# Order of the routing decision: exponentials ahead of the one-hot, gates one unit behind the ranks

## The chip, the cores and the metric

The kernel runs on one core of one Trainium2 chip. The metric is the device time of one execution in microseconds. The core has a matrix engine (PE, with its weight loads listed apart as PEld), a vector engine (DVE), a scalar engine (ACT), GpSimd (POOL) and a queue engine (SP) that issues most transfers.

## What is computed

Attention inside clusters, followed by a mixture of experts. There are 4 batches of 768 tokens with 8 heads of 64 columns; every token then has 512 features, and there are 3072 tokens.

```python
q_assign = argmax(q_n @ c_n); k_assign = argmax(k_n @ c_n)     # 16 clusters a head
scores   = where(q_assign == k_assign, scale * q @ k.T, -1e9)
x        = softmax(scores) @ v                                 # [3072, 512]

g_logits = x @ w_group                     # 4 groups
g_idx, g_w = argmax(g_logits), softmax(g_logits)[g_idx]
e_logits = x @ w_expert[g_idx]             # 4 experts in the group
e_idx, e_w = argmax(e_logits), softmax(e_logits)[e_idx]
out[token] = g_w * e_w * (relu(x @ w1[g, e]) @ w2[g, e])       # F = 1024
```

## The kernel before

**Attention** is cut into units: 32 heads with 9 units each, one unit being 512 columns of scores. In each unit PE makes the fine scores (tile `psf`, lines 346 and 347), ACT takes their exponential (`p`, L351), POOL subtracts the rounded part of it (`pl`, L353), and five units later PE multiplies both with V (L372 and L373). Beside that run coarse scores (`psc`, L304) for a head further ahead, whose maxima DVE takes (L307). All other work is hung beside units: `beside(g)` runs the jobs that are due in unit `g`, and a generator that says `yield` goes on one unit later. Generators that take a bank of the pool `psm` queue for turns. What is written in one unit is put into each engine's stream by a scheduler, so the order within a unit is not the order of the code.

**Routing.** When a batch's last head is done, `logits` multiplies its rows with the router's weights (L596 transposes, L604 products, L610 sums into `lg`: 6 blocks of 128 tokens, 20 logits each). Then `decide` runs for the batch. It takes the maxima of each 4 logits (`rmx`, L628), marks the first maximum (`req` L630 and L631, `rmw` L633, `roh` L635), multiplies group and expert to the one-hot of 16 experts (`roe`, L643), lets PE count with it how many earlier tokens chose each expert (L655 to L659, into `psm`), and adds that rank to the expert's start (`rps`, `rds`). The result `rdi` (L667) is each token's row in a table in HBM. Beside that it makes the gate: differences to the maxima (`rdf`, L638), exponentials (L639 on ACT), their sums (`rse`), and the reciprocal into `pay` (L650). Each of a batch's six table writes (L678, an indirect transfer issued by POOL) carries `pay` to the rows in `rdi`; they are issued one at a time, five units apart (four in the third batch).

**What hangs on the decisions.** After the third batch's decision (`then`) the generator `first` picks the fullest expert (L803 to L813), loads its weights (L760) from the number in `f0i`, splits them beside the units (L780 to L788), and, when all three batches' table writes have landed, reads that expert's rows of the table (`tabA`, L836), turns them into indices on DVE (`idA`, L842) and gathers the tokens with POOL (L916). The last batch's decision comes after attention, beside the first expert's products (L954, L976). Its table writes must land before SP reads the table (`tb`, L1096), behind which the other experts' weights wait in SP's queue (L760).

The lines that place the work are these:

```python
yield PSM, 1, 1            # a turn for a bank of psm, one unit on
...
if early: early()          # last batch: the experts' order
if then: then()            # third batch: starts first()
for c in range(T):
    for _ in range(1 if early else 4 if then else 5):
        yield
    ... nc.gpsimd.indirect_dma_start(out=self.table, ...)
```

Of the kernel before, what the change touches and what calls it, by code (L numbers as in the profile page):

```python
# [13 lines left out]
F32 = mybir.dt.float32  # L14
I32 = mybir.dt.int32
AF = mybir.ActivationFunctionType
ALU = mybir.AluOpType
AX = mybir.AxisListType
# [4 lines left out]
P = 128  # L23
SQ = 16.0
XS = 128.0
WS = 32.0
YS = 64.0
WRS = 16.0
# [500 lines left out]
class Router:  # L529
# [90 lines left out]
    def decide(self, b, early=None, then=None):  # L620
        nc, sm, E = self.nc, self.sm, self.E
        lg = self.lg[b]
        T = lg.shape[1]
        t0 = b * T
        G = T * 5
        lv = lg.rearrange("p t (g x) -> p (t g) x", x=4)
        mx = sm.tile([P, G], F32, name="rmx")
        nc.vector.tensor_reduce(out=mx, in_=lv, axis=AX.X, op=ALU.max)  # L628
        eq = sm.tile([P, G, 4], F16, name="req")
        nc.vector.tensor_tensor(out=eq, in0=lv, in1=mx.broadcast_to([P, G, 4]), op=ALU.is_ge)  # L630
        nc.vector.tensor_tensor(out=eq, in0=eq, in1=self.desc[:, 0:G], op=ALU.mult)  # L631
# [2 lines left out]
        oh = sm.tile([P, T, 5, 4], F16, name="roh")  # L634
        nc.vector.tensor_tensor(out=oh.rearrange("p t g x -> p (t g) x"), in0=eq, in1=mw.broadcast_to([P, G, 4]), op=ALU.is_equal)  # L635
        yield
        df = sm.tile([P, G, 4], F32, name="rdf")
        nc.vector.tensor_tensor(out=df, in0=lv, in1=mx.broadcast_to([P, G, 4]), op=ALU.subtract)  # L638
        nc.scalar.activation(out=df, in_=df, func=AF.Exp, scale=1.0 / (XS * WRS))  # L639
        se = sm.tile([P, T, 5], F32, name="rse")  # L640
        nc.vector.tensor_reduce(out=se.rearrange("p t g -> p (t g)"), in_=df, axis=AX.X, op=ALU.add)
        oe = sm.tile([P, T, 4, 4], F16, name="roe")
        nc.vector.tensor_tensor(out=oe, in0=oh[:, :, 1:5], in1=oh[:, :, 0].broadcast_to([P, T, 4, 4]), op=ALU.mult)  # L643
        ss = sm.tile([P, T, 4], F32, name="rss")
        nc.vector.tensor_tensor(out=ss, in0=se[:, :, 1:5], in1=oh[:, :, 0], op=ALU.mult)
        es = sm.tile([P, T], F32, name="res")
        nc.vector.tensor_reduce(out=es, in_=ss, axis=AX.X, op=ALU.add)
        nc.vector.tensor_scalar(out=es, in0=es, scalar1=1e-9, scalar2=None, op0=ALU.add)
        nc.vector.scalar_tensor_tensor(out=es, in0=se[:, :, 0], scalar=1e-9, in1=es, op0=ALU.add, op1=ALU.mult)
        nc.vector.reciprocal(out=self.pay[:, t0:t0 + T, 1], in_=es)  # L650
        yield PSM, 1, 1
        o16 = oe.rearrange("p t g x -> p (t g x)")
        rk = self.psm.tile([P, 512], F32, name="psm")
# [12 lines left out]
        di = sm.tile([P, T], I32, name="rdi", bufs=2)  # L666
        self.last["v"] = nc.vector.tensor_copy(out=di, in_=ds_)  # L667
        nc.vector.tensor_tensor(out=self.cb, in0=rk[:, W:W + E], in1=self.cb, op=ALU.add)
        if early:
            early()  # L670
        if then:
            then()
        for c in range(T):
# [3 lines left out]
            with self.tc.issue_after(self.cfg["lo"].ins) if self.apart and not early and "lo" in self.cfg else ExitStack():  # L677
                d = self.last["p"] = nc.gpsimd.indirect_dma_start(  # L678
                    out=self.table, out_offset=bass.IndirectOffsetOnAxis(ap=di[:, c:c + 1], axis=0),
                    in_=self.pay[:, t0 + c], in_offset=None)  # L680
# [756 lines left out]
```

## Time and profile before

| | |
|---|---|
| Three runs | 776.68, 778.99, 779.47 us (median 778.99) |
| Profiled execution | 779.44 us |
| Its span, first to last instruction | 777.2 us |
| Outside the span | 2.24 us |
| PE, PEld | 730.4 us (94%), 626.4 us (81%) |
| DVE, ACT, POOL | 606.1 (78%), 466.0 (60%), 492.1 us (63%) |
| Attention, then the last decision, then experts | about 0 to 426, 426 to 445, 445 to 777 us |

Busy time is a sum over the whole span, and different stages have different limits. A row of the timeline has start, duration, engine, line, operation, output and input, and in brackets how long the engine sat idle before it and what ended that idle time. Durations of neighbours on one engine overlap a little, since the next instruction begins before the one ahead has written its last result.

### The profile page before, as it was taken

To read this page: it belongs to the slowest core of one execution; us is meant where nothing else is said; L and a number is where in the kernel's file an instruction comes from. 1 tells how busy PE (TensorE), PEld (TensorE's weight loads), DVE (VectorE), ACT (ScalarE), POOL (GpSimd) and SP (SyncE) were. 2 spreads that over 40 slices of the span, in tenths; PEclk is the share of its full clock that TensorE was granted. 3 is DMA by queue.
4 is the path that set the end of the run, shared out by engine and by line. 5 is a ranking of instruction groups with operands and counts; after the bars stand their busy time and mean duration, and the time that the engine had idled before them with its cause. 6 is when DMAs were issued, how large, how long until landed. Compare 5 with 4: busy or idle time off the path is not lost. (4 is left out here: it accounts for less than half of the span.)

```text
span 777.2 us, 26716 instructions
## 1 busy us (share of the span) xinstructions
PE 730.4 (94%) x11086; PEld 626.4 (81%) x11086; DVE 606.1 (78%) x1209; ACT 466.0 (60%) x910; POOL 492.1 (63%) x522
## 2 busy tenths in 40 slices
PE   5899999999999999997989899999999999999992
PEld 3667888878888788886878687888789999999991
DVE  5888978899788998988875466857678888888840
ACT  5557877868777687775885255453444455555440
POOL 9567688779977799776972445434654555565330
PEclk9889999999999999999999999999999999999996
DMA  8756524535344352223312397876688788888700
GB/s 245 199 139 179 145 80 117 166 94 146 91 117 155 94 149 69 55 94 128 93 29 81 86 300 242 271 229 215 210 267 257 226 282 264 266 276 268 228 31 18
DMA packets 80392, 128.28 MB, mean 165 GB/s; under 512 B 8851, under 2 KB 47251, under 8 KB 80264
## 3 DMA queue, kind: packets, MB, share of 16 engines
q1 hardware_dynamic: 74492, 113.12, 48.9%
q0 software_dynamic: 5616, 13.35, 5.1%
q8 instruction: 88, 1.44, 0.8%
q14 instruction: 40, 0.33, 0.2%
q10 hardware_dynamic: 156, 0.03, 0.0%
HBM read 93.20 MB, written 14.11 MB: 138 GB/s over the span
## 5 line engine op out<-in xcount | busy, mean ns | idle before, releaser
L353 POOL TENSOR_TENSOR pl<-p 128x512 f16<-128x512 f32 x278 | 286.0, 1048 | 84.0 <-ACT p L351 79.5
L307 DVE TENSOR_REDUCE mpart<-psc 128x1 f32<-128x512 f32 (+1 forms) x282 | 189.9, 683 | 34.1 <-PE psc L304 34.1
L351 ACT ACTIVATE p<-psf 128x512 f32<-128x512 f32 x288 | 168.5, 594 | 56.4 <-PE psf L347 52.0
L372 PE MATMUL pso<-V,p 128*128 128x65 f16 x1152 | 161.9, 194 | 0.0
L372 PE MATMUL pso<-V,pl 128*128 128x65 f16 x1152 | 161.4, 194 | 0.0
L373 PE MATMUL pso<-V,pl 128*128 128x64 f16 x1152 | 161.2, 192 | 0.0
L373 PE MATMUL pso<-V,p 128*128 128x64 f16 x1152 | 161.1, 192 | 0.0
L346 PE MATMUL psf<-A 82*128 82x384 f16 (+2 forms) x576 | 145.5, 278 | 5.6 <-ACT p L351 4.8
L347 PE MATMUL psf<-B 128*128 128x384 f16 (+2 forms) x576 | 146.0, 278 | 0.0
L373 PEld LDWEIGHTS <-p 128*128 128x128 bf16 x1152 | 112.6, 98 | 21.6 <-issue 0.4
L372 PEld LDWEIGHTS <-p 128*128 128x128 bf16 x1152 | 112.1, 97 | 8.8 <-issue 0.8
L304 PE MATMUL psc<-A 80*128 80x512 f16 (+1 forms) x376 | 109.4, 332 | 4.1 <-DVE mpart L307 2.9
L373 PEld LDWEIGHTS <-pl 128*128 128x128 f16 x1152 | 112.8, 98 | 0.4
L372 PEld LDWEIGHTS <-pl 128*128 128x128 f16 x1152 | 111.2, 97 | 0.3
L957 DVE SCALAR_TENSOR_TENSOR hl<-psh,hh 128x160 f16<-128x160 f32 (+14 forms) x136 | 50.0, 371 | 61.2 <-ACT hh L956 61.0
L956 ACT ACTIVATE hh<-psh 128x160 f16<-128x160 f32 (+14 forms) x136 | 46.4, 346 | 66.5 <-PE psh L954 66.0
L954 PE MATMUL psh<-xT,wh0a 128*128 128x288 f16 (+7 forms) x512 | 74.7, 255 | 0.0
L347 PEld LDWEIGHTS <-B 128*128 128x128 f16 x576 | 57.2, 99 | 16.4 <-issue 8.0
L916 POOL DMA_INDIRECT xg<-xbuf,ri x32 | 40.9, 1279 | 39.6 <-PE psm L926 24.9
L954 PE MATMUL psh<-xT,wh0b 128*128 128x272 f16 (+6 forms) x448 | 65.0, 254 | 0.6 <-ACT xT L928 0.4
L346 PEld LDWEIGHTS <-A 82*128 82x128 f16 x576 | 56.1, 99 | 9.9 <-issue 1.0
L954 PE MATMUL psh<-xT,wl0a 128*128 128x288 f16 (+7 forms) x256 | 64.1, 255 | 0.0
(311 smaller groups left out, 1747.5 us busy)
## 6 DMA issues: line engine op xcount, KB each, us to landing
st<-w SPq DMA_DIRECT2D x128, 512.0 KB
B<-parts SPq DMA_DIRECT2D x64, 192.0 KB
kx<-kT SPq DMA_DIRECT2D x16, 384.0 KB
qx<-qT SPq DMA_DIRECT2D x16, 384.0 KB
vx<-vr SPq DMA_DIRECT2D x16, 384.0 KB
A<-parts SPq DMA_DIRECT2D x32, 192.0 KB
xbuf<-xs SPq DMA_DIRECT2D x4, 1536.0 KB
A<-mk SPq DMA_DIRECT2D x56, 24.0 KB
```

Source lines behind the costliest of these rows:

```text
L304: last["mm"] = nc.tensor.matmul(out=pc[:, off:off + k1 - k0], lhsT=QA[h % 8][0:80, c * P:(c + 1) * P], rhs=KA[h % 8][0:80, k0:k1], start=T ...
L307: nc.vector.tensor_reduce(out=(mp[:, 0, 0:1], mp[:, :, 1], mp[:, 1, 0:1])[i], in_=pc.rearrange("p (a x) -> p a x", a=n), axis=AX.X, op=ALU ...
L346: nc.tensor.matmul(out=o, lhsT=KA[h % 8][0:82, ks], rhs=QA[h % 8][0:82, q0:q1], start=True, stop=False)
L347: nc.tensor.matmul(out=o, lhsT=KBs[h][:, ks], rhs=QBs[h][:, q0:q1], start=False, stop=True)
L351: cfg["exp"] = nc.scalar.activation(out=p32, in_=pf, func=AF.Exp, scale=QK / (SQ * SQ))
L353: lo = (nc.vector if u in (EARLY if h < 2 else DVE_LO[h % 8] if h < NH - 2 else DVE_END) else nc.gpsimd).tensor_tensor(out=pl, in0=p32, in ...
L372: nc.tensor.matmul(out=O[:, col:col + 65], lhsT=p[:, bs], rhs=vh, start=c == 0 and q == 0 and i == 0, stop=False, skip_group_check=True)
L373: nc.tensor.matmul(out=O[:, col:col + 64], lhsT=p[:, bs], rhs=vl, start=False, stop=c == NCH - 1 and i == 1, skip_group_check=True)
L916: self.got = nc.gpsimd.indirect_dma_start(out=xg[0:n].rearrange("p a d -> p (a d)"), out_offset=None, in_offset=bass.IndirectOffsetOnAxis( ...
L954: self.mm = nc.tensor.matmul(out=ph[:, 0:M], lhsT=w[:, k, fs], rhs=xT[:, a, k], start=i == 0, stop=i == 3 * KD - 1)
L956: nc.scalar.activation(out=hh[:, f], in_=ph[:, 0:M], func=AF.Relu)
L957: self.ev = nc.vector.scalar_tensor_tensor(out=hl[:, f], in0=ph[:, 0:M], scalar=0.0, in1=hh[:, f], op0=ALU.max, op1=ALU.subtract)
```

## The change

In `decide`, the differences `rdf` and their exponentials move up, ahead of the comparisons. The sums, the product with the group's one-hot and the reciprocal (`rse`, `rss`, `res`, `pay`) move down behind the ranks, behind a new `yield`; `early()`, `then()` and the table writes follow them. No instruction is added or taken away, and the steps that make the one-hot from the comparisons stay as they are.

```diff
         nc.vector.tensor_reduce(out=mx, in_=lv, axis=AX.X, op=ALU.max)
+
+        df = sm.tile([P, G, 4], F32, name="rdf")
+        nc.vector.tensor_tensor(out=df, in0=lv, in1=mx.broadcast_to([P, G, 4]), op=ALU.subtract)
+        nc.scalar.activation(out=df, in_=df, func=AF.Exp, scale=1.0 / (XS * WRS))
         eq = sm.tile([P, G, 4], F16, name="req")
...
         yield
-        df = sm.tile([P, G, 4], F32, name="rdf")
-        nc.vector.tensor_tensor(out=df, in0=lv, in1=mx.broadcast_to([P, G, 4]), op=ALU.subtract)
-        nc.scalar.activation(out=df, in_=df, func=AF.Exp, scale=1.0 / (XS * WRS))
-        se = sm.tile([P, T, 5], F32, name="rse")
-        nc.vector.tensor_reduce(out=se.rearrange("p t g -> p (t g)"), in_=df, axis=AX.X, op=ALU.add)
         oe = sm.tile([P, T, 4, 4], F16, name="roe")
         nc.vector.tensor_tensor(out=oe, in0=oh[:, :, 1:5], in1=oh[:, :, 0].broadcast_to([P, T, 4, 4]), op=ALU.mult)
-        ss = sm.tile([P, T, 4], F32, name="rss")
-        nc.vector.tensor_tensor(out=ss, in0=se[:, :, 1:5], in1=oh[:, :, 0], op=ALU.mult)
-        es = sm.tile([P, T], F32, name="res")
-        nc.vector.tensor_reduce(out=es, in_=ss, axis=AX.X, op=ALU.add)
-        nc.vector.tensor_scalar(out=es, in0=es, scalar1=1e-9, scalar2=None, op0=ALU.add)
-        nc.vector.scalar_tensor_tensor(out=es, in0=se[:, :, 0], scalar=1e-9, in1=es, op0=ALU.add, op1=ALU.mult)
-        nc.vector.reciprocal(out=self.pay[:, t0:t0 + T, 1], in_=es)
         yield PSM, 1, 1
...
         nc.vector.tensor_tensor(out=self.cb, in0=rk[:, W:W + E], in1=self.cb, op=ALU.add)
+        yield
+
+        se = sm.tile([P, T, 5], F32, name="rse")
+        nc.vector.tensor_reduce(out=se.rearrange("p t g -> p (t g)"), in_=df, axis=AX.X, op=ALU.add)
+        ss = sm.tile([P, T, 4], F32, name="rss")
+        nc.vector.tensor_tensor(out=ss, in0=se[:, :, 1:5], in1=oh[:, :, 0], op=ALU.mult)
+        es = sm.tile([P, T], F32, name="res")
+        nc.vector.tensor_reduce(out=es, in_=ss, axis=AX.X, op=ALU.add)
+        nc.vector.tensor_scalar(out=es, in0=es, scalar1=1e-9, scalar2=None, op0=ALU.add)
+        nc.vector.scalar_tensor_tensor(out=es, in0=se[:, :, 0], scalar=1e-9, in1=es, op0=ALU.add, op1=ALU.mult)
+        nc.vector.reciprocal(out=self.pay[:, t0:t0 + T, 1], in_=es)
         if early:
             early()
```

On DVE, the third batch's decision stands so before, from the maxima to the one-hot (`mpart` are the coarse maxima of L307):

```order
L628 TENSOR_REDUCE rmx<-lg 128x30
L630 TENSOR_TENSOR req<-lg,rmx 128x120
L307 TENSOR_REDUCE mpart_199<-psc 128x2
L631 TENSOR_TENSOR req<-req,desc_502 128x120
L638 TENSOR_TENSOR rdf<-lg,rmx 128x120
L633 TENSOR_REDUCE rmw<-req 128x30
L635 TENSOR_TENSOR roh<-req,rmw 128x120
L307 TENSOR_REDUCE mpart_199<-psc 128x1
L641 TENSOR_REDUCE rse<-rdf 128x30
L643 TENSOR_TENSOR roe<-roh 128x96
```

and so in the changed kernel, whose lines have other numbers:

```order
L628 TENSOR_REDUCE rmx<-lg 128x30
L631 TENSOR_TENSOR rdf<-lg,rmx 128x120
L307 TENSOR_REDUCE mpart_199<-psc 128x2
L634 TENSOR_TENSOR req<-lg,rmx 128x120
L664 TENSOR_REDUCE rse<-rdf 128x30
L635 TENSOR_TENSOR req<-req,desc_502 128x120
L637 TENSOR_REDUCE rmw<-req 128x30
L307 TENSOR_REDUCE mpart_199<-psc 128x1
L639 TENSOR_TENSOR roh<-req,rmw 128x120
L642 TENSOR_TENSOR roe<-roh 128x96
```

`rdf` and `rse` have moved up past the comparisons, but both still stand ahead of `roe`: the same ten instructions in another order. The first two batches read alike.

On DVE, behind the same batch's ranks, `first` stands so before (`ft`, `cntA` and `fm` are its small tiles of 16 experts, `DEN`, `rec` and `pso` belong to the attention head that has just ended):

```order
L667 CAST rdi<-rds 128x6
L803 TENSOR_TENSOR cntA<-cb,ebase 128x16
L388 RECIPROCAL rec<-DEN 128x6
L804 SCALAR_TENSOR_TENSOR ft<-cntA,io 128x16
L391 TENSOR_TENSOR pso<-pso,rec 128x6x64
L805 TENSOR_REDUCE fm<-ft 128x1
L307 TENSOR_REDUCE mpart_199<-psc 128x1
L393 TENSOR_TENSOR xs<-pso,xs 128x6x64
```

and so in the changed kernel:

```order
L659 CAST rdi<-rds 128x6
L671 RECIPROCAL pay<-res 128x6
L388 RECIPROCAL rec<-DEN 128x6
L806 TENSOR_TENSOR cntA<-cb,ebase 128x16
L391 TENSOR_TENSOR pso<-pso,rec 128x6x64
L307 TENSOR_REDUCE mpart_199<-psc 128x1
L393 TENSOR_TENSOR xs<-pso,xs 128x6x64
L807 SCALAR_TENSOR_TENSOR ft<-cntA,io 128x16
```

`pay` has come in behind `rdi`, and two of `first`'s operations have moved behind the coarse maximum. On POOL, each batch's first table write stands one L353 later than before (behind 101 of them instead of 100 in the first batch), with the same spacing behind it, while the gather of L916 keeps its place: between the third batch's sixth write and that gather there are three L353 instead of four. SP's order is the same.

On DVE, the last decision stands so before, from the expert's `hl` (L957) on:

```order
L957 SCALAR_TENSOR_TENSOR hl<-psh,hh 128x288
L649 SCALAR_TENSOR_TENSOR res<-rse,res 128x6
L662 TENSOR_TENSOR rps<-psm,cb 128x96
L650 RECIPROCAL pay<-res 128x6
L663 TENSOR_TENSOR rps<-rps,roe 128x96
L668 TENSOR_TENSOR cb<-psm,cb 128x16
L665 TENSOR_REDUCE rds<-rps 128x6
L1051 TENSOR_TENSOR c_11405<-cb,ebase 128x16
L1087 COPY pb<-pay 128x6
L667 CAST rdi<-rds 128x6
```

and so in the changed kernel:

```order
L960 SCALAR_TENSOR_TENSOR hl<-psh,hh 128x288
L654 TENSOR_TENSOR rps<-psm,cb 128x96
L669 TENSOR_SCALAR res<-res 128x6
L655 TENSOR_TENSOR rps<-rps,roe 128x96
L660 TENSOR_TENSOR cb<-psm,cb 128x16
L657 TENSOR_REDUCE rds<-rps 128x6
L670 SCALAR_TENSOR_TENSOR res<-rse,res 128x6
L1054 TENSOR_TENSOR c_11405<-cb,ebase 128x16
L659 CAST rdi<-rds 128x6
L671 RECIPROCAL pay<-res 128x6
```

The second multiplication of the gate (`res` from `res`) has moved from ahead of `hl` to behind it, `pay` now comes directly behind `rdi`, and the copy `pb` has gone further down.

## Rows read from the trace of the kernel before

**Rows 1.** The page, part 1: the span, and each engine's busy time, share and instructions.

```profile
span 777.2 us, 26716 instructions
PE 730.4 (94%) x11086; PEld 626.4 (81%) x11086; DVE 606.1 (78%) x1209; ACT 466.0 (60%) x910; POOL 492.1 (63%) x522
```

**Rows 2.** PE's waits over the whole span: what waited, for what, us in total, times, longest.

```profile
PE psm L655 <- DVE roe L643: 4.1, 3, 1.4
PE psc L304 <- DVE mpart L307: 2.9, 6, 0.8
...
PE psm L1126 <- DMA tb<-table: 2.8, 1, 2.8
```

**Rows 3.** The timeline of PE between 340 and 372 us, the rows with idle time before them.

```profile
350.70 0.20 PE L655 MATMUL psm<-roe,low 128*128 128x96 f16 x1 [1.35 <-DVE roe L643]
...
355.83 0.38 PE L304 MATMUL psc<-A 80*128 80x256 f16 x2 [0.73 <-DVE mpart L307]
360.17 0.38 PE L304 MATMUL psc<-A 80*128 80x256 f16 x2 [0.69 <-DVE mpart L307]
365.15 0.27 PE L346 MATMUL psf<-A 82*128 82x256 f16 x1 [1.53 <-ACT p L351]
```

**Rows 4.** The timeline of DVE in the third batch's decision.

```profile
346.43 0.85 DVE L630 TENSOR_TENSOR req<-lg,rmx 128x120 f16<-128x120 f32 x1
...
347.80 0.45 DVE L631 TENSOR_TENSOR req<-req,desc 128x120 f16<-128x120 f16 x1
348.18 0.27 DVE L638 TENSOR_TENSOR rdf<-lg,rmx 128x120 f32<-128x120 f32 x1
...
348.67 0.82 DVE L635 TENSOR_TENSOR roh<-req,rmw 128x120 f16<-128x120 f16 x1
...
350.19 0.45 DVE L643 TENSOR_TENSOR roe<-roh 128x96 f16<-128x96 f16 x1
```

**Rows 5.** The timeline of POOL in the same stretch: five L353 in a row.

```profile
345.10 5.43 POOL L353 TENSOR_TENSOR pl<-p 128x512 f16<-128x512 f32 x5 [1.03 <-ACT p L351]
```

**Rows 6.** The same operations and the exponential in all four decisions: count, shortest, median and longest in ns, first and last start in us. The shortest is that of the last decision, in which POOL runs no L353.

```profile
L630 DVE TENSOR_TENSOR req<-lg,rmx x4: 284/852/856, 155.1 to 426.0; 128x120 f16<-128x120 f32 x4
L631 DVE TENSOR_TENSOR req<-req,desc x4: 215/452/452, 156.5 to 426.4; 128x120 f16<-128x120 f16 x4
...
L635 DVE TENSOR_TENSOR roh<-req,rmw x4: 274/816/817, 157.3 to 427.0; 128x120 f16<-128x120 f16 x4
...
L643 DVE TENSOR_TENSOR roe<-roh x4: 257/454/454, 158.9 to 427.3; 128x96 f16<-128x96 f16 x4
...
L639 ACT ACTIVATE rdf<-rdf x4: 303/303/303, 157.1 to 426.5; 128x120 f32<-128x120 f32 x4
```

**Rows 7.** The timeline of DVE behind the third batch's ranks.

```profile
353.65 0.98 DVE L804 SCALAR_TENSOR_TENSOR ft<-cntA,io 128x16 f32<-128x16 f32 x1
...
355.10 0.67 DVE L307 TENSOR_REDUCE mpart<-psc 128x1 f32<-128x512 f32 x1
...
358.34 0.97 DVE L812 TENSOR_TENSOR ft<-ft,oh 128x16 f32<-128x16 f32 x1
...
359.44 0.68 DVE L307 TENSOR_REDUCE mpart<-psc 128x1 f32<-128x512 f32 x1
```

**Rows 8.** ACT and POOL where the first expert's weights arrive.

```profile
363.03 1.06 ACT L780 ACTIVATE wh<-st 128x1024 f16<-128x1024 f32 x1 [1.50 <-DMA st<-w]
364.00 0.58 ACT L787 ACTIVATE psm<-st 128x512 f32<-128x512 f32 x1
...
365.17 2.04 POOL L353 TENSOR_TENSOR pl<-p 128x512 f16<-128x512 f32 x2 [2.00 <-ACT p L351]
```

**Rows 9.** The third batch's sixth table write, the reading of the table and what hangs on it, on POOL, SP, DVE and PE; then the time to landing of all 24 table writes.

```profile
388.26 0.98 POOL L678 DMA_INDIRECT table<-pay,rdi  x1 [0.17 <-issue]
390.67 1.45 SPq L836 DMA_DIRECT2D tabA<-table  x3
392.44 0.15 DVE L842 CAST idA<-tabA 128x1 int32<-128x1 f32 x1 [1.85 <-DMA tabA<-table]
...
393.07 0.15 DVE L842 CAST idA<-tabA 128x1 int32<-128x1 f32 x1 [0.42 <-DMA tabA<-table]
...
393.44 0.20 DVE L610 TENSOR_TENSOR lg<-psm,lg 128x60 f32<-128x60 f32 x1
393.69 0.50 PE L596 MATMUL psm<-ident,xs 128*128 128x128 f16 x6 [1.16 <-DVE lg L610]
...
DMA to landing us min/median/max: 2.1/3.8/7.6
```

**Rows 10.** The last decision on DVE, its first table write on POOL, and SP's reading of the table.

```profile
428.61 0.18 DVE L650 RECIPROCAL pay<-res 128x6 f32<-128x6 f32 x1
...
429.19 0.17 DVE L1051 TENSOR_TENSOR c<-cb,ebase 128x16 f32<-128x16 f32 x1
429.27 0.17 DVE L1087 COPY pb<-pay 128x6 f32<-128x6 f32 x1
429.34 0.17 DVE L667 CAST rdi<-rds 128x6 int32<-128x6 f32 x1
...
429.79 1.02 POOL L678 DMA_INDIRECT table<-pay,rdi  x1 [9.34 <-DVE st L1091]
...
442.10 0.35 SPq L1096 DMA_DIRECT2D tb<-table  x1
```

## The prediction

> **What bounds the kernel now.** I read the page first: PE is busy for 730.4 of 777.2 us, so an edit on DVE, ACT or POOL can only move the time where PE waits for it [rows 1]. The list of PE's waits comes next, because it says what such places are worth. The only wait of PE for a decision is L655 for `roe`: 4.1 us in three times, one per batch inside attention [rows 2]. The timeline of PE around the third one shows where the change's other effects must land: 1.35 us for `roe`, then 0.73 and 0.69 us for coarse maxima that stand behind `first`'s arithmetic on DVE, then 1.53 us for exponentials that stand behind the arriving weights on ACT [rows 3]. Last come the two places where a table write is on the path: the third batch's table, for which DVE and then PE wait [rows 9], and the last batch's, behind which the experts' weights start [rows 10] and for which PE waits 2.8 us [rows 2].
>
> **Part 1: `roe` in the first three batches.** The 4.1 us would shrink if fewer instructions stood ahead of `roe`. The order shows the same ten, so their sum is unchanged and only their waits can differ. Those waits are visible: the four operations with two inputs in SBUF take 0.85, 0.45, 0.82 and 0.45 us [rows 4] where they take 0.284, 0.215, 0.274 and 0.257 us without L353 beside them [rows 6]. The excess is 0.57, 0.24, 0.55 and 0.19, together 1.55 us. `rdf`, which stands directly behind one of them, takes only 0.27 [rows 4]. So an operation with two inputs seems to wait until the current L353 lets go. End minus unheld duration gives the moments of release: 347.0, 348.04, 349.22 and 350.38 us; from the end of one held operation, or of the `rdf` behind it, to the next release it is about 0.77 us, while five L353 take 5.43 us [rows 5].
>
> The Trainium skill, "SBUF — State Buffer", section "Who interferes with whom", says that a vector instruction with two SBUF inputs contends with a GpSimd instruction that reads SBUF, that the one that starts first has the port for the whole instruction, and that reductions do not contend. The trace agrees, with 0.85 against 0.284 us for the same `req`. That rule speaks against this edit, since `rdf` now comes first and takes the wait without bringing `roe` nearer.
>
> I walk the new order against the same POOL. `rdf` waits for 347.0 and ends at 347.27; the coarse maximum runs to 347.87; `req` waits for 348.04 and ends at 348.32; `rse` fits into the next hold; the second `req` is held until 348.32 + 0.77 = 349.09 and ends at 349.31; `rmw` and a coarse maximum take until 350.2, past the release at about 350.1; `roh` ends at about 350.4 and `roe`, with no sixth L353 behind, at 350.68. Before, `roe` ended at 350.64. So the term is +0.05 us for each batch, **+0.15** for three. The bounds are one hold less for each batch (3 x -0.57 = -1.7) and one more (3 x +0.77 = +2.3). I take the value walked, because the phase of POOL is fixed by PE's pace and was the same in all three (the medians and longest of rows 6 agree). The exponential on ACT moves ahead of one L351; it takes 0.3 us [rows 6] at a time when ACT idles and PE waits for `roe` anyway, so I count nothing for it. If that cover failed, it would cost at most those 0.3 us a batch.
>
> **Part 2: the third batch's `first`.** L804 takes 0.98 us for 16 columns, where L1051 of the same width takes 0.17 [rows 7, 10]: again a hold. Before it stood ahead of the coarse maximum that PE waits for at 355.83; now that maximum stands ahead of it, with only `pay` (0.18 us) new in front. So it ends some 0.8 us sooner and the wait of 0.73 goes. The next wait, 0.69 at 360.17, follows a sum of DVE work that has only been reordered, L812 with its 0.97 us included, so it need not go. The gain lies between 0 and 1.4 us; I take the middle, **-0.6**. The weights' number `f0i` comes at about the same time, and on ACT an L351 now stands directly behind the first L780, where L787 with 0.5 us to the next start stood between [rows 8]; so the wait of 1.53 us at 365.15 does not grow and the 0.6 passes through it, and POOL resumes about 0.6 sooner than 365.17 [rows 3, 8].
>
> **Part 3: the third batch's table.** The six writes come one unit, thus one L353, later. From 365.17 on POOL has no idle time to make that up, so the sixth write starts at 388.26 + 1.03 - 0.6 = 388.7. SP reads the table 2.4 us behind it, DVE waits at `idA` and PE at L596 [rows 9]. DVE's wait therefore ends at 392.9 instead of 392.44. `L610`, for which PE waits, now stands behind one pair of `idA` and `gA` instead of three, so it starts at about 393.1 instead of 393.44, but the coarse maximum behind the second pair at about 393.7 instead of 393.57. PE is thus tied to the table again and what part 2 won is given back: **+0.6**. Bounds: 0 (the table is not the later of the two) and +1.03 (a whole L353, with nothing won before).
>
> **Part 4: the last decision.** Here POOL does not contend. The path from `rmx` to `roe` loses its filler (`rdf` and a reduction stood between dependent operations; `rdi` starts 0.1 us before the copy ahead of it ends [rows 10], which an operation that needs the one ahead cannot): two such places less some overlap, +0.14 us by adding up starts. Behind `hl`, which waits for ACT anyway, the step `res` has gone from ahead of it, and the copy `pb` of 0.17 us no longer stands before `rdi`; but the write now needs `pay`, one instruction behind `rdi`. Adding up starts, `pay` ends at about 429.53 where `rdi` ended at 429.51, so the first table write keeps its 429.79 [rows 10]: **0.0**. All that follows, tb at 442.10 and the weights behind it in SP's queue, shifts by whatever this is. Bounds: -0.17 (the copy's place) and +0.45 (`rps` held behind a later `hl`).
>
> **Sum:** +0.15 - 0.6 + 0.6 + 0.0 = +0.15 us on the profiled execution's 779.44, thus 779.6. That execution lies 0.45 above the median of the runs, 778.99, so the forecast for a median is 779.1.
>
> **The rivals.** About 0.5% (3.9 us) is what a measurement here can tell from no change: below 775.1 is faster, above 782.9 slower.
>
> *The one-hot comes sooner.* If `roe` were ready when PE arrives, the whole 4.1 us would go: 779.0 - 4.1 = 774.9. For it speaks that this wait is the largest that a decision causes; against it, that the same ten instructions stand ahead of `roe`. The change as worded does not happen to the one-hot at all. A part of it, one hold less in each batch, or part 2 kept, gives 776 to 778.
>
> *More holds on the shared port.* With POOL in another phase, each decision pays one more hold: 779.1 + 2.2 = 781.3. For it speaks that `rdf` newly takes a hold ahead of `req`; against it the walk above. The Trainium skill's rule, "SBUF — State Buffer", section "Who interferes with whom", taken alone and without the phases, would make this the outcome; the trace bears out the hold, not yet the number of holds.
>
> *The table comes late.* The sixth write now leaves later, and its landing took 2.4 us where others took up to 7.6 [rows 9]. If it lands as slowly as the slowest, DVE stands 5.2 us longer with coarse maxima, `L610` and weight splits behind it, and PE with it: 779.1 + 5.2 = 784.3. From 3.8 us of extra wait it decides the sign. Against it: nothing of the transfer itself has changed.
>
> *The gate becomes last in the last decision.* `pay` behind `hl` and `rdi` by 0.45 us or more: 779.6 and up, with everything behind tb.
>
> **How the numbers follow.** Forecast 0.72 (own range 778.0 to 780.4: the run-to-run spread and half of the bounds of parts 2 and 3); sooner one-hot in part 0.08, in full 0.04; more holds 0.08; late table 0.05; late gate 0.03. The range of 776.2 to 782.2 takes in the forecast, the partial gain, the holds and the late gate, and leaves out about 0.1 to 0.15. Faster than 775.1: the full gain and a little of the partial one, 0.05. Slower than 782.9: the late table and the tails of the holds, 0.08. The rest, 0.87, is no measurable change.
>
> **What would show it.** Part 1 is right if L655 still waits about 1.4 us three times, and if `rdf` now takes about 0.8 us and the second `req` about 0.9. Part 2: the wait near 355.8 is gone. Part 3: the sixth table write starts 0.2 to 1 us later, DVE waits longer for `tabA`, and `L610` stands behind one pair. Part 4: the first write of the last batch starts within 0.3 us of 429.8. The prediction is wrong if `roe`'s wait falls by more than 0.6 us a batch, if PE waits for `tabA`'s chain by 3 us more, or if the experts' stage behind 445 us, which the edit does not touch, changes its length.

## The result: slower by 0.7%, and the profile after

The changed kernel took 784.43 us (median of 10 runs, 780.2 to 788.08), the kernel before 778.80 us in the same comparison: a ratio of 1.0073, with a 95% interval of 1.005 to 1.0096. The prediction of 779.1 us lies below it, and so does its whole range. The profiled execution took 784.45 us, with a span of 782.3 against 777.2. One run of last_only below (1045.98 us) was in a slow state and is left out.

The page, part 1, and three of PE's waits over the whole span (what waited, for what, us in total, times, longest) read in the changed kernel:

```profile
span 782.3 us, 26718 instructions
PE 733.9 (94%) x11086; PEld 628.2 (80%) x11086; DVE 604.5 (77%) x1209; ACT 467.3 (60%) x910; POOL 497.3 (64%) x522
```

```profile
PE psm L647 <- DVE roe L642: 4.8, 3, 1.6
...
PE psc L304 <- DVE mpart L307: 2.6, 6, 0.8
PE psm L1129 <- DMA tb<-table: 3.6, 1, 3.6
```

The wait for `roe` grew from 1.36 to 1.59 us a batch [rows 2, 3], by 0.7 us in all, and the wait for `tb` by 0.8. But PE's busy time grew too, by 3.5 us for the same 11086 products [rows 1], and in attention alone by 3.7. A slower clock is one thing that makes products take longer. Over the whole span PE's granted clock is no lower than before (0.982 of full speed against 0.979), so the place has to be looked for: in attention it is 0.991 against 1.00. The third batch shows where. First PE's rows with idle time between 352 and 369 us, then the stretch behind the wait in windows of 1 us (window, length, busy share and count of PE, PEld, DVE, ACT and POOL, then PE's granted clock as a share of 2.4 GHz, DMA share and GB/s):

```profile
352.46 0.20 PE L647 MATMUL psm<-roe,low 128*128 128x96 f16 x1 [1.59 <-DVE roe L642]
362.33 0.38 PE L304 MATMUL psc<-A 80*128 80x256 f16 x2 [0.41 <-DVE mpart L307]
367.19 0.27 PE L346 MATMUL psf<-A 82*128 82x256 f16 x1 [1.40 <-ACT p L351]
```

```profile
353.00:354.00 1.00, 1.00 (x23) 0.93 (x22) 0.97 (x8) 0.50 (x1) 0.00 (x0) 1.00 0.00 0
354.00:355.00 1.00, 1.00 (x9) 0.49 (x6) 1.00 (x4) 0.11 (x2) 0.83 (x1) 0.54 0.00 0
355.00:356.00 1.00, 1.00 (x18) 0.89 (x17) 1.00 (x6) 0.58 (x1) 0.56 (x2) 0.50 0.00 0
356.00:357.00 1.00, 1.00 (x9) 0.64 (x7) 1.00 (x2) 0.48 (x1) 0.70 (x1) 0.50 0.00 0
357.00:358.00 1.00, 1.00 (x20) 0.73 (x18) 0.68 (x3) 0.60 (x1) 0.20 (x1) 0.75 0.00 0
```

PE idles for 1.59 us, starts again, and 1.6 us later its granted clock drops from 2.4 to 1.2 GHz and stays there for some 3.4 us. I call this a fall. It happens behind the first batch's wait as well (159.5 to 162.9 us), not behind the second's. In the kernel before the same place reads 1.00 throughout, as do the other two batches:

```profile
351.00:352.00 1.00, 1.00 (x24) 0.92 (x21) 0.97 (x5) 0.27 (x1) 0.00 (x0) 1.00 0.00 0
352.00:353.00 1.00, 1.00 (x22) 0.74 (x19) 1.00 (x5) 0.44 (x2) 0.59 (x1) 1.00 0.00 0
353.00:354.00 1.00, 1.00 (x23) 0.74 (x19) 1.00 (x6) 0.49 (x1) 0.88 (x2) 1.00 0.00 0
```

Each fall costs 1.7 us of full clock (3.4 x 0.5).

One execution also varies by itself, so the result was split by stage. There is one L351 a unit, which gives the same point of the work in every trace. *Start* runs to the seventeenth L351, *attention* from there to the last, *seam* from there to the first product with `tb`, *tail* from there to the end. Five profiles of the changed kernel (the first is the one above, the others are experiments below) stand against two of the kernel before, in us:

| profile | start | attention | falls in it | seam | tail | span |
|---|---|---|---|---|---|---|
| before | 54.0 | 363.1 | 0 | 26.9 | 333.1 | 777.2 |
| before_again | 50.5 | 365.7 | 2 | 26.8 | 333.1 | 776.1 |
| after | 52.1 | 367.0 | 2 | 29.7 | 333.5 | 782.3 |
| after_again | 52.4 | 363.5 | 0 | 29.1 | 332.7 | 777.7 |
| after_third | 51.5 | 364.2 | 1 | 28.9 | 333.6 | 778.1 |
| after_fourth | 50.8 | 364.4 | 1 | 29.2 | 332.3 | 776.8 |
| after_fifth | 52.8 | 365.6 | 1 | 28.3 | 335.2 | 781.9 |

Between the first profiles before and after, attention grew by 3.9 us and the seam by 2.7. Between the means of two and of five, the seam grew by 2.1 and attention by 0.5, with before_again's two falls in it. What a fall costs on the path shows when the products of two profiles of the changed kernel are matched one by one: past each of the five falls PE is 1.16 to 1.35 us further behind after_again, which has none, than it was ahead of the fall. From the 89th to the 113th L351, around the first batch's decision, the profiles with a fall there take 1.2 to 1.4 us longer than after_again; after_fifth takes 1.1 us longer there without one, so falls are not the only thing that differs. The start, which the edit does not reach, varies by 3.5 us. The two falls in before_again are not behind `roe` but behind waits of PE for L351 (1.67 and 1.38 us).

### The profile page after: what moved, and what is told of

It reads as the page before. It is cut to its first block, busy times and chain, and to the rows that moved or that the text cites. A ratio compares the mean times of both kernels' runs of the same rounds, so it can differ in the third digit from the quotient of the medians.

```text
span 782.3 us, 26718 instructions
## 1 busy us (share of the span) xinstructions
PE 733.9 (94%) x11086; PEld 628.2 (80%) x11086; DVE 604.5 (77%) x1209; ACT 467.3 (60%) x910; POOL 497.3 (64%) x522
## 5 line engine op out<-in xcount | busy, mean ns | idle before, releaser
L353 POOL TENSOR_TENSOR pl<-p 128x512 f16<-128x512 f32 x278 | 286.6, 1049 | 85.8 <-ACT p L351 81.9
L307 DVE TENSOR_REDUCE mpart<-psc 128x1 f32<-128x512 f32 (+1 forms) x282 | 190.1, 683 | 34.7 <-PE psc L304 33.8
L351 ACT ACTIVATE p<-psf 128x512 f32<-128x512 f32 x288 | 169.3, 595 | 58.6 <-PE psf L347 52.5
L957 PE MATMUL psh<-xT,wh0a 128*128 128x288 f16 (+7 forms) x512 | 74.7, 255 | 0.0
L957 PE MATMUL psh<-xT,wh0b 128*128 128x272 f16 (+6 forms) x448 | 65.0, 254 | 0.1
L957 PE MATMUL psh<-xT,wl0a 128*128 128x288 f16 (+7 forms) x256 | 64.0, 255 | 0.0
```

What stands on the lines that cost most here:

```text
L307: nc.vector.tensor_reduce(out=(mp[:, 0, 0:1], mp[:, :, 1], mp[:, 1, 0:1])[i], in_=pc.rearrange("p (a x) -> p a x", a=n), axis=AX.X, op=ALU ...
L351: cfg["exp"] = nc.scalar.activation(out=p32, in_=pf, func=AF.Exp, scale=QK / (SQ * SQ))
L353: lo = (nc.vector if u in (EARLY if h < 2 else DVE_LO[h % 8] if h < NH - 2 else DVE_END) else nc.gpsimd).tensor_tensor(out=pl, in0=p32, in ...
L957: self.mm = nc.tensor.matmul(out=ph[:, 0:M], lhsT=w[:, k, fs], rhs=xT[:, a, k], start=i == 0, stop=i == 3 * KD - 1)
```

## Experiments

Runs under one heading shared a chip and the runs of the kernel before there. The ratios in brackets are those on record; they can differ from the quotient of the two medians by some 0.001 (after_third: 1.0015 and 1.0026).

### The edit in parts

*exp_only*, the kernel before with its three lines of `rdf` moved up:

```diff
         nc.vector.tensor_reduce(out=mx, in_=lv, axis=AX.X, op=ALU.max)
+        df = sm.tile(...); subtract; exp      # moved up
```

> Only the differences and exponentials move up; gates stay where they were in the kernel before. Theory A (the wait for roe grew from 1.36 to 1.59 us a batch, and TensorE's granted clock falls to its lower level for some 3.3 us behind it, which the trace of the changed kernel shows in two of three batches): the reordered DVE instructions ahead of roe are all here, so the waits are again near 1.6 us, the clock is 0.5 for about 3 us behind one to three of them, and the time is 782 to 784.5 us. Theory B (the last decision and its landing at the seam): the gate is not behind the rank here, so 779 to 780 us. Theory C (the new unit ahead of the gates, with first and the table behind it): 779 us.

*gates_only*, the changed kernel with these lines back behind the first `yield`:

```diff
         yield
+        df = sm.tile(...); subtract; exp      # back in the unit of roe
         oe = sm.tile([P, T, 4, 4], F16, name="roe")
```

> Only the gates move behind the ranks, with the new unit; exponentials stay one unit behind the comparisons. Theory A (waits for roe and the clock): one DVE instruction (rse) fewer stands ahead of roe, so the wait is 1.2 to 1.36 us, the clock stays at 1.00 behind it, and the time is 778 to 779.5 us. Theory B (gate last at the seam): 781 to 784 us, lost behind 430 us. Theory C (unit, first and table): 781 to 784 us, lost between 352 and 426 us.

*three_batches* and *last_only* hold both versions of `decide`:

```diff
+        return (self.decide_new if b < 3 else self.decide_old)(b, early, then)
```

with `b == 3` in the second.

> The changed decision in the three batches inside attention, the old one in the last batch. Theory A: 782 to 784.5 us, with waits for roe of 1.6 us and low clock behind some. Theory B (seam): 778.5 to 780 us. Theory C: 782 to 784 us without a fall of the clock in attention.

> The old decision in the three batches inside attention, the changed one in the last batch. Theory A: attention is as in the kernel before (waits of 1.36 us, clock 1.00), time 778 to 780 us. Theory B (seam): 781.5 to 784.5 us, with the first experts' table read 2 to 3 us later against the end of attention. Theory C: 779 us.

Measured, beside 778.62 before: exp_only 783.99 us (1.0072, 1.0047 to 1.0096), gates_only 779.08 (1.0001, 0.998 to 1.0023), three_batches 779.53 (1.0015, 0.9996 to 1.0035), last_only 780.53 (1.0015, 0.9992 to 1.0037). The wait for `roe` is 1.59 us wherever the exponentials have moved up, 1.35 where not; falls behind it: one in exp_only, one in three_batches, none in the other two. So it is the exponentials that lengthen the wait. But the parts do not add up: three_batches holds all of the change in attention and loses 0.9 us, exp_only 5.4; last_only, which holds all of it in the last decision, is not clear of the kernel before either. Two causes had to be separated, the falls and something of exp_only's own. Its trace shows the second, on SP, POOL, ACT and PE where the first expert's weights arrive:

```profile
360.09 2.12 SPq L760 DMA_DIRECT2D st<-w  x4
...
359.34 0.98 POOL L678 DMA_INDIRECT table<-pay,rdi  x1 [0.15 <-DVE ft L811]
...
366.57 1.06 ACT L780 ACTIVATE wh<-st 128x1024 f16<-128x1024 f32 x1 [4.92 <-DMA st<-w]
...
368.68 0.37 PE L346 MATMUL psf<-A 82*128 82x256 f16 x1 [4.95 <-ACT p L351]
```

In the kernel before, SP and POOL read:

```profile
359.24 2.13 SPq L760 DMA_DIRECT2D st<-w  x4
...
359.44 0.99 POOL L678 DMA_INDIRECT table<-pay,rdi  x1 [0.16 <-DVE ft L812]
```

Before, the weights are issued 0.20 us ahead of the batch's first table write, and ACT has them 3.8 us later [rows 8]. In exp_only, counted from `rmx`, the weights are issued 0.33 us later (13.45 instead of 13.12 us), since `f0i` is, and the write 0.63 us earlier (12.69 instead of 13.32): it is now 0.75 us ahead of the weights, and they take 6.5 us. ACT waits for them with the next L351 queued behind, so PE waits 4.95 us where it waited 1.53 [rows 3], and two more falls come at 368 us, in this wait, and at 409. In the windows 363:364 and 364:365 of exp_only the transfers move 39 and 29 GB/s, where those of the kernel before move 300 to 400.

### The wait filled, or avoided

*after_again* is the changed kernel itself.

> The changed kernel once more, beside the others of this call. Theory A (waits for roe of 1.59 us, behind each of which the clock may fall for 3.4 us, at a cost of 1.7 us): three waits of 1.59 us again, since they repeat to 0.01 us, but the falls of the clock sit behind other waits than last time; 782.5 to 785.5 us. Theory N (the first result was an unlucky set of runs): 778.5 to 781 us.

*after_fill* (`fz` is a tile of zeros; the bank is overwritten by the rank products):

```diff
+        for _ in range(0 if early else 7):
+            nc.tensor.matmul(out=rk, lhsT=self.ones, rhs=self.fz, start=True, stop=True, skip_group_check=True)
         nc.tensor.matmul(out=rk[:, 0:W], lhsT=self.low, rhs=o16, start=True, stop=False, skip_group_check=True)
```

> The changed kernel with seven idle products of 512 columns by a zero tile (about 1.5 us) put ahead of the rank products of the three batches inside attention, where PE waits for roe. Nothing becomes ready sooner. Theory A: PE does not pause there, the wait named roe shrinks to 0.1 to 0.3 us, the granted clock stays at 1.00 behind it, and the time falls by the clock's part alone, 1.5 to 4 us, to 780 to 782.5 us. Theory W (the wait itself and what DVE and POOL do costs the time, not the clock): 784 us as without the filler. Theory S (the loss is behind attention): 784 us as well, with clock 1.00 in attention.

*after_later* and *before_later*, on the changed kernel and on the one before:

```diff
-        yield PSM, 1, 1
+        yield PSM, 2, 1
         o16 = oe.rearrange("p t g x -> p (t g x)")
```

> The changed kernel with the rank products one unit later in the three batches (table writes too, then). Theory A: no wait for roe, no fall of the clock behind it; it loses all that the longer waits cost and the 4.1 us of before as well: 775 to 779 us. Theory S (the loss is at the last decision and the seam): 779 to 781 us, that is 4.8 us less than the changed kernel. Theory C (a table one unit later still holds up PE near 390 us): 780 to 784 us.

> The kernel before with the rank products one unit later in the three batches. Theory A: its three waits of 1.36 us go, 4.1 us, and the clock already stood: 774.5 to 776 us. Theory C (the third batch's table one unit later gives it back): 776 to 779 us.

Measured, beside 778.24: after_again 780.08 us (1.0025, 1.0001 to 1.0048), after_fill 784.61 (1.0082, 1.0054 to 1.0109), after_later 782.35 (1.0048, 1.0017 to 1.0079), before_later 776.58 (0.998, 0.9957 to 1.0002). The changed kernel has the same waits of 1.58 and 1.59 us and not one fall behind them, and its attention is 3.5 us shorter than in the first profile. With the filler there is no wait and no fall at `roe`, but the time does not drop; it is near the 784 us that was forecast for a cost without the clock. But something else was added: in its new order ACT takes a second copy (L200) ahead of the next exponential, and PE waits 1.14 us for that. It says nothing on the price of the clock. In after_later a wait of 0.62 us is left, and falls come with later waits of 2.17 and 2.85 us in the third batch. In before_later the waits are gone, attention is 2.9 us shorter than in the first profile of the kernel before, and no fall occurs in it.

### The wait alone

*after_third* is the changed kernel again.

> The changed kernel a third time, on the chip of this call. The two profiles so far have the same waits for roe (1.58 and 1.59 us) and differ in the clock behind them: two falls in one (784.4 us), none in the other (780.1 us). Theory A (the falls follow the waits of 1.59 us by chance, one in three so far): 779 to 785 us, and the profiled run is longer than 778 by 1.7 us for each fall that its trace shows in attention. Theory L (something else differs between the loads of the program): a profiled run that is slow or fast without falls to match.

*before_slow1* and *before_slow4* lengthen the wait in the kernel before (n is 1 and 4):

```diff
+        for _ in range(0 if early else n):
+            oc = sm.tile([P, T, 5, 4], F16, name="roc", bufs=2)
+            nc.vector.tensor_copy(out=oc, in_=oh)
+            oh = oc
         oe = sm.tile([P, T, 4, 4], F16, name="roe")
```

> The kernel before, with one copy of the one-hot on DVE between the one-hot and roe in the three batches, the order otherwise the same; the waits for roe grow from 1.36 to about 1.55 us, as in the changed kernel, without any of its edits. Theory A: now and then a fall of the clock behind roe as in the changed kernel, 779.5 to 782.5 us. Theory W (only the wait counts): 0.6 us more than before, 778.6 to 779.4. Theory E (it is the place of the edits that costs, not the wait): the same as W.

> The same with four copies: waits for roe of 2.4 to 2.9 us. Theory A: falls of the clock behind two or three of the three waits, 1.7 us each, on top of 3.1 to 4.6 us of longer waits: 784.5 to 788.5 us. Theory W: the longer waits alone, 781.5 to 783.5 us, with clock 1.00 behind them.

*onehot_first* (`exps` holds the subtraction and the exponential, `ro` is the product into `oe`):

```diff
+        if not early:
+            with self.tc.issue_after(ro.ins):
+                exps()
```

> The changed kernel, but in the three batches the differences and exponentials are held behind roe, so that nothing but the comparisons stands ahead of it. The wait for roe should fall from 1.59 to 0.6 to 1.1 us. Theory A: no fall of the clock behind it, and 1.5 to 3 us less waiting: 775.5 to 778.5 us. Theory S (what the change costs lies in the last decision, which is as in the changed kernel): 2 us less than the changed kernel of this call at most, 778 to 782 us.

Measured, beside 778.17: after_third 780.17 us (1.0015, 0.9996 to 1.0033), before_slow1 783.29 (1.0058, 1.0031 to 1.0085), before_slow4 790.48 (1.0148, 1.0119 to 1.0178), onehot_first 780.82 (1.0031, 1.0013 to 1.0049). One copy makes the wait 1.58 us, and with it come a fall behind the first batch's wait and, as in exp_only, a table write 0.74 us ahead of weights that then take 6.1 us: nothing of the edit is needed for either. The time lies above the 779.5 to 782.5 us expected, which had no late weights in it. With four copies all three waits are 2.40 us and all three are followed by a fall; the write is 0.85 us ahead of the weights here too, so its time, above the 784.5 to 788.5 us expected, holds that cost as well. The third fall looks like this on PE and in the clock:

```profile
357.34 0.20 PE L659 MATMUL psm<-roe,low 128*128 128x96 f16 x1 [2.40 <-DVE roe L647]
```

```profile
357.00:358.00 1.00, 0.66 (x23) 0.66 (x23) 0.94 (x4) 0.00 (x0) 0.00 (x0) 1.00 0.00 0
358.00:359.00 1.00, 1.00 (x16) 0.62 (x13) 1.00 (x10) 0.00 (x0) 0.00 (x0) 0.74 0.00 0
359.00:360.00 1.00, 1.00 (x17) 0.87 (x16) 1.00 (x5) 0.99 (x2) 0.32 (x1) 0.50 0.00 0
```

In onehot_first the wait is 1.27 us with no fall, but PE then waits 1.11 us for a coarse maximum, in the first batch here and in the second alike, with DVE's work behind `roe` in another order:

```profile
156.93 0.20 PE L653 MATMUL psm<-roe,low 128*128 128x96 f16 x1 [1.27 <-DVE roe L645]
163.72 0.38 PE L304 MATMUL psc<-A 80*128 80x512 f16 x1 [1.11 <-DVE mpart L307]
```

### Table writes behind the weights, and one instruction less

*after_fourth* is the changed kernel, *before_again* the one before.

> The changed kernel a fourth time. Theory A: the waits for roe are 1.59 us again; over the four profiles of it about one fall for three waits; the profiled run is near 779.5 us and 1.7 us more for each fall in attention; median 779.5 to 784.5 us. Theory L: the profiled run does not follow the number of falls.

> The kernel before itself. Waits for roe of 1.35 us and clock 1.00 behind them in all theories; weights of the first expert 3.8 us from issue to use; 777.5 to 779.5 us. It tells how far the end of attention and the table's landing at the seam vary by themselves.

*exp_yield* is exp_only and one line:

```diff
         nc.vector.tensor_tensor(out=self.cb, in0=rk[:, W:W + E], in1=self.cb, op=ALU.add)
+        yield
```

> Exponentials moved up, gates as in the kernel before, and the new unit behind the ranks, so that table writes and the first expert's choice come one unit later. Theory D (a table write issued ahead of the first expert's weights makes them land 2.4 us later, and ACT's exponentials and PE behind it wait 3.5 us longer): the third batch's first table write is issued 2 to 3 us behind the weights, these land 3.6 to 4.0 us after their issue, PE's wait near 365 us is 1.3 to 1.6 us, and the time is 779.5 to 781.5 us. Theory G (gates ahead of the ranks cost it, with late exponentials): 783 to 785 us as with the exponentials alone.

*after_rse* holds `rse` behind `roe`:

```diff
+        with ExitStack() if early else self.tc.issue_after(ro.ins):
             nc.vector.tensor_reduce(out=se.rearrange("p t g -> p (t g)"), in_=df, axis=AX.X, op=ALU.add)
```

> The changed kernel with the sums rse held behind roe in the three batches, so that one instruction less of 0.26 us stands ahead of it. The wait for roe shrinks from 1.59 to 1.35 to 1.45 us, about that of the kernel before. Theory A: no falls behind it, 778 to 779.5 us, at least 1 us less than the changed kernel of this call. Theory S (the cost is the last decision): no less than 0.5 us under it.

Measured, beside 778.16: after_fourth 779.52 us (1.0022, 1.0003 to 1.0042), before_again 778.74 (1.0011, 0.9986 to 1.0035), exp_yield 778.90 (1.001, 0.9991 to 1.0029), after_rse 780.89 (1.0036, 1.0016 to 1.0056). With the one `yield` the loss against the kernel before of the same comparison is 0.7 us, where exp_only lost 5.4. Its SP, POOL and ACT show why:

```profile
357.14 2.13 SPq L761 DMA_DIRECT2D st<-w  x4
...
359.70 0.98 POOL L679 DMA_INDIRECT table<-pay,rdi  x1
...
361.65 1.06 ACT L781 ACTIVATE wh<-st 128x1024 f16<-128x1024 f32 x1 [2.74 <-DMA st<-w]
```

The table write now comes 2.56 us behind the weights, which take 4.5 us (3.6 to 4.0 was expected). The Trainium skill, "DMA: Bandwidth & Descriptors", section "Issuing engines are not separate DMA queues", says that transfers of SP and POOL run on the same 16 engines and interleave. The order of these two issues and what it costs the weights agree with that.

In after_rse the wait stays at 1.58 us. A wait of 1.35 to 1.45 us was expected. The second `req` starts 0.07 us sooner there, takes 0.97 us instead of 0.90, and ends at the same point, 3.21 us from the start of `rmx`: the next release of L353 sets it, and `rse` had stood inside that hold.

### One more chip

> The changed kernel a fifth time. If the first set stands alone: 779 to 781 us, 1 to 2.5 us over the kernel before of this call, with none to two falls of the clock behind waits of 1.59 us. If sets like the first are common: 783 to 786 us.

> The kernel before with the rank products one unit later in the three batches, a second time. No wait for roe, clock 1.00 in attention: 775.5 to 777.5 us, 1.5 to 2.5 us under the kernel before of this call. If the first gain was chance: 777.5 to 779.5 us.

Measured, beside 780.28: after_fifth 784.50 us (1.0053, 1.0028 to 1.0079), before_later2 779.57 (1.0003, 0.998 to 1.0027). The first set does not stand alone, then: over the kernel before of its own comparison the changed kernel lost 5.6, 1.8, 2.0, 1.4 and 4.2 us, 3.0 on average. The gain of before_later did not repeat (775.5 to 777.5 us was expected), so no version here is shown to beat the kernel before.

### Falls behind the decisions of all profiles

| PE's wait for `roe` | kernels | waits | followed by a fall |
|---|---|---|---|
| 0 to 0.62 us | before_later, before_later2, after_fill, after_later | 12 | 0 |
| 1.27 us | onehot_first | 3 | 0 |
| 1.35 to 1.36 us | before, before_again, gates_only, last_only | 12 | 0 |
| 1.58 to 1.59 us | the five of the changed kernel, exp_only, exp_yield, three_batches, before_slow1, after_rse | 30 | 10 |
| 2.40 us | before_slow4 | 3 | 3 |

If 1.35 and 1.59 us were alike, 10 falls among 42 waits would leave those 12 without one in about 2 of 100 cases. The length does not decide alone: of 25 other waits of PE in attention, of 1.38 to 2.25 us, four were followed by a fall (1.38, 1.39, 1.67 and 2.17 us).

## Why the prediction was wrong, by its own steps

**Part 1 (+0.15 forecast, +0.7 measured, and the falls left out).** The walk over POOL's releases held until its last step but one. These are DVE's rows in the third batch, and POOL's:

```profile
347.95 0.85 DVE L631 TENSOR_TENSOR rdf<-lg,rmx 128x120 f32<-128x120 f32 x1
...
349.33 0.52 DVE L634 TENSOR_TENSOR req<-lg,rmx 128x120 f16<-128x120 f32 x1
349.77 0.27 DVE L664 TENSOR_REDUCE rse<-rdf 128x30 f32<-128x120 f32 x1
349.95 0.90 DVE L635 TENSOR_TENSOR req<-req,desc 128x120 f16<-128x120 f16 x1
...
351.68 0.44 DVE L639 TENSOR_TENSOR roh<-req,rmw 128x120 f16<-128x120 f16 x1
352.15 0.26 DVE L642 TENSOR_TENSOR roe<-roh 128x96 f16<-128x96 f16 x1
```

```profile
346.63 4.15 POOL L353 TENSOR_TENSOR pl<-p 128x512 f16<-128x512 f32 x4 [1.02 <-ACT p L351]
350.94 1.04 POOL L353 TENSOR_TENSOR pl<-p 128x512 f16<-128x512 f32 x1 [0.16 <-ACT p L351]
```

`rdf` took 0.85 us (0.8 forecast), the second `req` 0.90 (0.9 forecast), `rse` cost nothing. The step that failed is "`rmw` and a coarse maximum take until 350.2, past the release at about 350.1". The fifth L353 starts 0.16 us behind the end of the fourth, for its input, so its release comes at 351.85, 4.21 us from `rmx`, where the walk had put about 4.0; `roh` is held by it and takes 0.44 us instead of 0.274. That is one more hold, of 0.17 us. The pause is not new: in the kernel before, the fifth L353 starts at 349.50, 0.15 us behind the fourth's end, inside the row of five [rows 5], and the prediction's own moments put 1.16 us between the last two releases (349.22 and 350.38), where the walk let 1.0 pass. The rule quoted from the Trainium skill, "SBUF — State Buffer", section "Who interferes with whom", agrees with this hold, and its direction was the right one.

The larger fault is that the sum priced a wait at its own length. A wait for `roe` of 1.35 us was followed by no fall in 12 cases, one of 1.59 us in 10 of 30. So 0.23 us more a batch brought one fall an execution on average (2, 0, 1, 1 and 1 in the five profiles), 1.2 to 1.4 us each. The prediction had no step for the clock. That a longer wait does it without the edit is shown by before_slow1 (one fall of three, at 1.58 us) and before_slow4.

**Part 2 (-0.6) held, part 3 (+0.6) did not.** The wait at 355.8 us is gone. The sixth table write left 39.1 us from the third `roe` instead of 37.6 [rows 3, 9], 1.3 us of it by the fall; in the four later profiles, which have none there, 37.7 to 38.0 us. DVE waited longer for the table, 2.47 us instead of 1.85. But the `lg` sum behind it kept PE waiting 0.91 us instead of 1.16:

```profile
391.55 0.99 POOL L681 DMA_INDIRECT table<-pay,rdi  x1 [0.17 <-issue]
393.83 1.45 SPq L839 DMA_DIRECT2D tabA<-table  x3
395.54 0.15 DVE L845 CAST idA<-tabA 128x1 int32<-128x1 f32 x1 [2.47 <-DMA tabA<-table]
...
395.68 0.21 DVE L610 TENSOR_TENSOR lg<-psm,lg 128x60 f32<-128x60 f32 x1
...
395.94 0.50 PE L596 MATMUL psm<-ident,xs 128*128 128x128 f16 x6 [0.91 <-DVE lg L610]
```

The pair of `idA` and `gA` that left from ahead of `lg` outweighed the later landing, so nothing was given back. In the four later profiles it took 42.1 to 42.4 us from `roe` to this product, before 43.0: the two parts together are worth -0.6 to -0.9, not 0.

**Part 4 (0.0) held for the write and failed behind it.** The first write came 1.97 us behind the rank products, before 2.16: a gain of 0.2, near the bound of -0.17, and the sixth a little more. "All that follows, tb at 442.10 and the weights behind it in SP's queue, shifts by whatever this is" is the step that failed. From the last write to SP's reading of `tb` it took 7.15, 6.78, 7.40, 6.86 and 7.14 us in the five profiles, 5.72 and 5.61 in the two of before. A weight load that SP issues between the writes shows what differs. In the kernel before, the fourth write and this load, and the window in which most of it moves:

```profile
433.86 0.96 POOL L678 DMA_INDIRECT table<-pay,rdi  x1 [0.31 <-issue]
...
434.16 0.39 SPq L760 DMA_DIRECT2D st<-w  x1
```

```profile
438.00:439.00 1.00, 1.00 (x11) 0.80 (x9) 0.00 (x0) 0.00 (x0) 1.00 (x3) 1.00 0.91 344
```

In after_again the fourth and the sixth write, the load, `tb`, and the windows at the same and at a later distance:

```profile
432.39 0.96 POOL L681 DMA_INDIRECT table<-pay,rdi  x1 [0.31 <-issue]
...
434.91 0.96 POOL L681 DMA_INDIRECT table<-pay,rdi  x1 [0.30 <-issue]
...
433.03 0.39 SPq L763 DMA_DIRECT2D st<-w  x1
441.69 0.35 SPq L1099 DMA_DIRECT2D tb<-table  x1
```

```profile
437.00:438.00 1.00, 1.00 (x11) 0.80 (x9) 0.00 (x0) 0.00 (x0) 1.00 (x1) 1.00 0.54 39
...
439.00:440.00 1.00, 1.00 (x9) 0.61 (x7) 0.00 (x0) 0.00 (x0) 0.00 (x0) 1.00 0.62 225
```

The fourth write leads the load by 0.30 us before and by 0.64 here, and the load's bytes come about 2 us later. It looks like the third batch's weights in small, but that is a likeness. Over 20 profiles of all kernels, a lead of 0.30 to 0.32 us (of the write last issued ahead of the load) goes with 5.6 to 7.0 us from the last write to `tb` (11 profiles, mean 6.2), one of 0.48 to 1.14 with 6.4 to 8.0 (9, mean 7.1). No run changed this lead alone, so for the seam it is an association. The whole seam took 29.0 us on average in the eleven profiles whose last decision has the gates behind the ranks (28.2 to 30.3), 27.8 in the nine others (26.8 to 29.3): 1.2 us.

**The rivals.** The late table, which gave 784.3 and so the nearest time, had the wrong place: the third batch's table held PE up no longer than before. More holds came true in kind, at 0.23 us a batch instead of 0.77. The late gate did not happen, since the first write left sooner.

**The sum, put right for an average execution:** waits for `roe` +0.7, parts 2 and 3 -0.8, falls +1.3, seam +1.2, together +2.4 us, against a mean loss of 3.0 us over the five comparisons. With the seam of the table, +2.1, it is 3.3. Either way it is added up from means; the 0.6 us or 0.3 us between is within what the start and the tail vary by, and the share of the seam is not shown by a run that changes it alone.

**What stays open:** why two chips lost 4 to 6 us and three 1.4 to 2.0. The first chip's profile has two falls in attention and a long seam, but after_fifth has only one fall, and its long start and tail (335.2 us) lie in stages that the edit does not touch. Part of it is in attention and not behind a fall: against after_again, PE loses 1.5 us between 180 and 290 us in the first profile and, beside its fall, 1.9 between 175 and 290 in after_fifth; after_third and after_fourth lose 0.4 to 0.5. Most of it begins where ACT and DVE start about half a microsecond late behind a product that is not late itself (267.8 and 280.6 us, 170.5 and 183.4). before_later2, without the edit and on the chip of after_fifth, loses 1.4 and 1.1 us against before_later in the same way, so the edit is not needed for it; what causes it is not known. And why the second table write takes POOL 0.98 us in most profiles with the changed last decision, but 1.21 and 1.22 in onehot_first and after_later, and 1.18 before; it is most of what moves the lead.

## What to carry to other kernels

A wait of the matrix engine need not be worth its length alone: here a quarter of a microsecond more, from 1.35 to 1.59 us, came with a further cost of 1.2 to 1.4 us in a third of the cases. Look at the granted clock behind each wait before a price is put on it. Where small scattered writes and a bulk load that someone waits for are issued within a microsecond of each other, their order is a term of the sum, and an edit that moves either by half a microsecond can turn it. Take apart a result of some tenths of a per cent by stage and over several profiles before explaining it, since a stage that the edit does not touch can vary by as much.

## What the runs showed of the hardware

- Behind a wait of PE for `roe` the granted clock fell from 2.4 to 1.2 GHz, 0.1 to 1.7 us after the wait had ended, and stayed there for 3.4 us each time. It fell in 10 of 30 cases at 1.59 us, in none of 12 at 1.35, in 3 of 3 at 2.40. Of 25 other waits in attention, of 1.38 to 2.25 us, four were followed by a fall.
- Where a table write was issued 0.74 to 0.85 us ahead of the weight load, the weights took 6.1 to 6.5 us instead of 3.6 to 4.5 (3 profiles against the 17 others), at 29 to 129 GB/s in the slowest windows of exp_only.
- A reduction on DVE between two held operations cost nothing: without it the next held operation ended at the same point (3.21 us from `rmx` with and without).
